# A first batch rearranged: the order of its steps, its filler matmuls, the banks they use, and two loads for the output weights

## The chip, the cores and the metric

One core of a Trainium2 chip runs the whole kernel. The core's engines work beside each other, each on its own list of instructions in a fixed order: TensorE (matmuls into the accumulator memory PSUM), VectorE (DVE in the profile), ScalarE (ACT), GpSimd (POOL, which issues most loads here) and SyncE (SP, which issues stores and transposing transfers). An instruction that needs another engine's result, or a buffer that another engine still reads, waits on a semaphore, and everything behind it on its own engine waits too. The metric is the device time of one execution in microseconds (us), as a median of several.

## The reference

The kernel computes Linformer attention and then a gated feed-forward layer. There are 8 batches, 8 heads of 64 and 1024 positions:

```python
k_proj = np.einsum('ks,bhsd->bhkd', E, k)
v_proj = np.einsum('ks,bhsd->bhkd', F, v)
scores = scale * np.matmul(q, k_proj.transpose(0, 1, 3, 2))
attn = softmax(scores)                        # over 64 projected positions
x = matmul(attn, v_proj)                      # as 8192 rows of 8 x 64 = 512
out = (sigmoid(x @ w_gate) * (x @ w_val)) @ w_out
```

E and F project 1024 positions to 64. w_gate and w_val are 512 x 1536, w_out is 1536 x 512. All inputs are float32; the kernel's loads turn them to bfloat16.

## The kernel before

The feed-forward layer is most of the work. It runs on blocks of 512 rows, two blocks to a batch, and its operand is xT, the attention's output transposed into four slices of 128 columns (i = 0 to 3). From the second batch on, a planner (`arranged`, L58) puts instructions in order by estimated costs and due times. The first batch, which the change touches, is written out by hand (L1865 to L2010): the order of the calls is the order on each engine.

The first batch's first block is handled in two halves of the heads, R = 0 (heads 0 to 3) and R = 1 (heads 4 to 7), since the loads come in halves. `start_loads` (L472) issues on GpSimd, in this order: k R=0, q R=0, k R=1, q R=1, v R=0, v R=1, then the weights in chunks. Loads are served one after the other. The steps of one half are:

- `k_part(R)`: `project` (16 matmuls with E into one bank), then `keep_k`, a cast to SBUF by ScalarE (L660).
- `qt(R, engines)`: q is transposed by TensorE into two banks, each copied out by the engine named (L715).
- `turn_k`: transposes the projected k, then a copy by ScalarE to kpD (L686).
- `sc(R)`: scores into two banks; ScalarE writes their exponentials to eT (L738).
- `den(R)`: sums of the exponentials by matmul with a selection matrix, then a RECIPROCAL on VectorE (L764, L780).
- `bc(R)`: spreads the reciprocals over partitions by float32 matmuls into two banks; the calls `keep(0)` and `keep(1)` let ScalarE copy them to xu (L797).
- `v_part(R)`: `project` with F into two banks, then four casts to vpD, two on ScalarE and two on VectorE (`keep_v`, L670).
- `xo(R)`: attention times v into two banks, then VectorE scales them by xu into xT (L843): two instructions of 512 columns for R = 0 (`scale`, L829), four of 256 for R = 1 (L869).

After these, `first_pair` (L1256) begins the feed-forward layer with the pair m = 0, 1 of its twelve column groups, on slices i = 0 and 1 (heads of R = 0), runs xo(1) in between, and goes on to slices 2 and 3. `mstep` and the rest follow; the output projection `oproj` (L1312) reads w_out (tile wO) first at 72.0 us. wO is one load, issued on GpSimd once two transposes of q have landed (L1912).

`busy(n)` (L628) issues n filler matmuls of 128x512. Their result is read by nobody; they go to PSUM bank F3, and like every writer of a bank they wait for whoever still reads what stood in it.

PSUM has eight banks, A0 to A3 and F0 to F3. In the first block the steps take banks from one list in the order of their calls, `whole` (L358); `first_pair` then uses F0 to F3. The program records for each bank who wrote and read it, and emits a wait where an engine comes to a bank that another has not yet finished with (`Plan.add`, L154).

```python
    + (A2, A3, F0, A0, A1, F1)      # the list before, its second line: k, q, q, turn_k, sc, sc
```

Of the kernel before, what the change touches and what calls it, by code (L numbers as in the profile page):

```python
# [12 lines left out]
P = 128  # L13
# [224 lines left out]
def bass_linformer_attn__then__ffn_glu_sigmoid_kernel(  # L238
# [18 lines left out]
    with contextlib.ExitStack() as es:  # L257
# [89 lines left out]
        class Ring:  # L347
# [9 lines left out]
        F0, F1, F2, F3 = FB  # L357
        whole = Ring(  # L358
            (A0, A1)
            + (A2, A3, F0, A0, A1, F1)  # L360
            + (A2, F2, A3, A0, F0)
            + (A2, A3, A1, F1, F2)
            + (A0, F0, A1, F1, A2, A3)
            + (A0, F3, A2, A3)
        )
        ffn, att = Ring(FB), Ring(AB)

# [289 lines left out]
                        tp=(0, 64 * h),  # L657
                    )

        def keep_k(bk, c0, R=None):  # L660
            width = 256 if R is None else 128
            act(
                kp[:, pairs(R), :],
                bank[bk][:, c0 : c0 + width],
                [],
                [("kp", x) for x in both(R)],
                b=bk,
            )

        def keep_v(bks, c0, engines, R=None):  # L670
            vv = vpD[:, :, :].rearrange("p (r h) d -> p r h d", h=2)
            width = 256 if R is None else 128
            for n, (h, g) in enumerate(((0, 0), (1, 1), (0, 1), (1, 0))):
                o = vv[64 * g : 64 * g + 64, pairs(R), h, :]
                i = bank[bks[h]][64 * h : 64 * h + 64, c0 : c0 + width].rearrange(
                    "p (r d) -> p r d", d=DH
                )
                ws = [("vpD", h, g, x) for x in both(R)]
                if engines[n] == "ACT":
                    act(o, i, [], ws, b=bks[h])  # L680
                else:
                    dve(lambda e, o=o, i=i: e.tensor_copy(o, i), [], ws, b=bks[h])  # L682

        def turn_k(ring, R=None):
            bk = ring.next()
            ob = bank[bk][:, :].bitcast(BF16)  # L686
            rs = range(NR)[pairs(R)]
            for n, r in enumerate(rs):
                for g in range(2):
                    mm(  # L690
                        bk,
                        ob[64 * g : 64 * g + 64, n * P : (n + 1) * P],
                        kp[:, r, :],
                        ident[:, :],
                        [("kp", r // 2), "ident"],
                        tr=True,
                        tp=(0, 64 * g),
                    )
            act(
                kpD[:, 2 * rs[0] : 2 * rs[-1] + 2, :].rearrange("p h c -> p (h c)"),  # L700
                ob[:, 0 : P * len(rs)],
                [],
                [("kpD", x) for x in both(R)],
                b=bk,
            )

        def VPD(R):
# [2 lines left out]
        def half_unit(hf, ring):  # L710
# [4 lines left out]
            def qt(R, engines):  # L715
                for rr, eng in enumerate(engines):
                    bk = ring.next()
                    ob = bank[bk][:, :].bitcast(BF16)
                    for x in range(2):
                        for t in range(2):  # L720
                            c = x * 2 + t
                            mm(
                                bk,
                                ob[:, c * P : (c + 1) * P],
                                Qb[:, 4 * R + 2 * rr + x, (2 * hf + t) * P : (2 * hf + t + 1) * P],
                                ident[:, :],
                                [("Q", hf, R), "ident"],
                                tr=True,
                            )
                    o = qv[:, R, 2 * rr : 2 * rr + 2, 256 * hf : 256 * hf + 256]  # L730
                    i = ob[:, 0:512].rearrange("p (x c) -> p x c", x=2)
                    ws = [("qT", hf, R, rr)]
                    if eng == "ACT":
                        act(o, i, [], ws, b=bk)
                    else:
                        dve(lambda e, o=o, i=i: e.tensor_copy(o, i), [], ws, b=bk)

            def sc(R):  # L738
                bks = [ring.next(), ring.next()]
# [103 lines left out]
            def xo(R):  # L843
                bks = [ring.next(), ring.next()]
                for rr in range(2):
                    for g in range(2):
                        for c in range(2):
                            h = 4 * R + 2 * rr + c
                            kk = slice(64 * (g ^ c), 64 * (g ^ c) + 64)
                            mm(  # L850
                                bks[g],
                                bank[bks[g]][64 * c : 64 * c + 64, 256 * rr : 256 * rr + 256],
                                vpD[kk, h, :],
                                eT[kk, 2 * R + g, 256 * rr : 256 * rr + 256],
                                VPD(R) + [("eT", 2 * R + g)],
                                tp=(64 * (g ^ c), 64 * c),
                            )
                for g in range(2):
                    n = 2 * R + g
                    if hf:  # L860
                        act(xu[:, n, :], bank[bks[g]][:, :], [], [("xu", n)], b=bks[g])
                    elif R == 0:
                        scale(R, g, bank[bks[g]], xu[:, n, :], [("xu", n)], bks[g])
                if hf == 0 and R == 1:
                    for r in (2, 3):
                        for g in range(2):
                            cc = slice(256 * (r - 2), 256 * (r - 2) + 256)
                            dve(
                                lambda e, r=r, g=g, cc=cc: e.tensor_tensor(  # L869
                                    xT[s][:, r, hf, 256 * g : 256 * g + 256],  # L870
                                    bank[bks[g]][:, cc],
                                    xu[:, 2 * R + g, cc],
                                    ALU.mult,
                                ),
                                [("xu", 2 * R + g)],
                                [("xT", s, r, hf, g)],
                                b=bks[g],
                            )
# [377 lines left out]
        def first_pair(blk, between):  # L1256
# [3 lines left out]
                for i in ii:  # L1260
                    mm_one(blk, m, i, n, pbs[m, n])

            step(0, "G", 0, 1)
            step(1, "G", 0, 1)
            if between:
                between()
            step(0, "V", 0, 1)
# [44 lines left out]
        def oproj(blk, tt, pb, cols=((0, DM),)):  # L1312
# [3 lines left out]
            for n, (c0, c1) in enumerate(cols):  # L1316
                if n:
                    pb = FF.take()
                for m in range(NF):
                    mm(  # L1320
                        pb,
                        bank[pb][:, 0 : c1 - c0],
                        hT[blk % 2][:, m, tt * P : (tt + 1) * P],
                        wO[:, m, c0:c1],
                        [("hT", blk % 2, m, tt // 2), "wO", "wO12"],
                        start=(m == 0),
                        stop=(m == NF - 1),
                    )
# [22 lines left out]
        def t_sums(n):  # L1351
# [1 line left out]
            B21, B22 = wO[:, H6:NF, 0:256], wO[:, H6:NF, 256:512]  # L1353
            T4, T3, T2 = [wT[:, i, :, :] for i in range(3)]
            o, a, b, op, r, w = {
                3: (T3, B22, B12, ALU.subtract, ["wO", "wO12"], [("wT", 3)]),
                2: (T2, T3, B11, ALU.add, ["wO", ("wT", 3)], [("wT", 2)]),
                4: (T4, B21, T2, ALU.subtract, ["wO", ("wT", 2)], [("wT", 4)]),
                1: (B12, B12, B11, ALU.subtract, ["wO"], ["wO12", ("wT", 1)]),
            }[n]  # L1360
            if n == 4:
                w = w + ["bsel8", ("kp", 0), ("kp", 1)]
# [28 lines left out]
        def product(blk, bk, A, B, start=False, stop=False, js=(0, 1), ms=(0, NF // 2), also=()):  # L1391
            h = hT[blk % 2]
            for j in js:
                for m in range(*ms):
# [7 lines left out]
                    elif B[0] == "T":  # L1402
                        rhs, k = wT[:, 4 - int(B[1]), m, :], ("wT", int(B[1]))
                    else:
                        c = 256 * (B[2] == "2")
                        rhs, k = wO[:, m + H6 * (B[1] == "2"), c : c + 256], "wO"
                    mm(
                        bk,
                        bank[bk][:, 256 * j : 256 * j + 256],
# [459 lines left out]
        busy(5)  # L1869
        qt, sc, den, bc, xo = half_unit(0, whole)  # L1870

        def k_part(R):
            bk = whole.next()
            project(0, 0, [bk, bk], 0, R)
            keep_k(bk, 0, R)

        def v_part(R):
            bks = [whole.next(), whole.next()]
            project(1, 1, bks, 0, R)
            keep_v(bks, 0, ["ACT", "DVE", "ACT", "DVE"], R)  # L1880

        k_part(0)
        qt(0, ("DVE", "DVE"))
        turn_k(whole, 0)
        busy(1)
        sc(0)
        busy(2)
        k_part(1)
        den(0)
        turn_k(whole, 1)  # L1890
        busy(1)
        qt(1, ("ACT", "DVE"))
        busy(1)
        sc(1)
        keep = bc(0)
        keep(0)
        keep(1)
        den(1)
        v_part(0)
        busy(1)  # L1900
        xo(0)
        keep = bc(1)
        keep(0)
        v_part(1)
        keep(1)

        def second_loads():
# [1 line left out]
            load_k(1)  # L1909
            load_v(1)  # L1910
            transpose_q()
            load(  # L1912
                wO[:, :, :],
                moe_w_out.rearrange("(m p) c -> p m c", p=P),
                ["wO", "wO12"],
                "wO",
                r=turned()[:2],
            )


        todo, at = [], {}
# [200 lines left out]
```

## Time and profile before

| what | value |
| --- | --- |
| median of 8 runs | 518.69 us (518.47 to 519.29) |
| the profiled execution's own time | 518.55 us |
| its span | 516.8 us |
| TensorE busy | 504.8 us (98%) |
| VectorE busy | 409.8 us (79%) |
| ScalarE busy | 345.5 us (67%) |
| first feed-forward matmul | starts at 21.98 us |
| load of w_out | issued at 57.37 us, 13.5 us to landing |

The span is the time between the first and the last instruction of the profiled execution; its own time includes what lies around that. Times of rows are counted from the span's start. A row has a group of equal instructions: the tile written, the tiles read, partitions by elements, and how many. The tiles' names leave numbers out, so that pA is any of A0 to A3 and pF any of F0 to F3. Some small tiles of the first batch live inside larger ones that are used later: the reciprocals and the identity matrix stand under gT, the projected k under wT, the selection patterns under vT.

### The profile page before, as it was taken

How to read it: one execution, taken by the hardware profiler on the slowest of the kernel's cores; microseconds unless marked ns; L12 is line 12 of the kernel's file. 1: busy time of each engine (PE TensorE's matmuls, PEld its weight loads, DVE VectorE, ACT ScalarE, POOL GpSimd, SP SyncE). 2: the span in 40 equal slices, each digit the busy share in tenths (PEclk: the TensorE clock that was granted, in tenths of full speed). 3: DMA queues.
4: the chain of work that ended last, by engine and by line, in shares of the span. 5: the costliest groups of instructions: out<-in, count | busy, mean ns of one | idle time of the engine just before them, and what ended most of it. 6: DMA issues, size and time to landing. Idle time of an engine off the chain costs nothing.

```text
span 516.8 us, 11359 instructions
## 1 busy us (share of the span) xinstructions
PE 504.8 (98%) x4595; PEld 410.4 (79%) x4595; DVE 409.8 (79%) x806; ACT 345.5 (67%) x646; POOL 40.4 (8%) x59
## 2 busy tenths in 40 slices
PE   4899999999999999999999999999999999999997
PEld 2545645888888888888888888888888888888885
DVE  4448789889779796987879887797968898786775
ACT  2565682867777767676767676777677766676752
POOL 9420201200200020000200020000000000000000
PEclk9999999999999999999999999999999999999999
DMA  9999999899599779364957379374104330201013
GB/s 166 199 199 203 149 199 211 121 177 223 79 214 171 162 134 155 63 160 127 158 87 163 63 139 205 67 154 92 64 1 103 42 103 1 82 2 62 20 42 124
DMA packets 105189, 63.13 MB, mean 122 GB/s; under 512 B 63024, under 2 KB 97328, under 8 KB 105136
## 3 DMA queue, kind: packets, MB, share of 16 engines
q0 software_dynamic: 33984, 29.89, 37.5%
q1 hardware_dynamic: 71152, 32.52, 28.3%
q8 instruction: 36, 0.59, 0.5%
q14 instruction: 17, 0.14, 0.1%
HBM read 60.29 MB, written 16.78 MB: 149 GB/s over the span
## 4 chain that ended last, share of the span: by engine, by line
PE 94%; DMA 2%; DVE 1%; ACT 1%; POOL 0%; issue 0%; DVEq 0%; POOLq 0%
PE pA L385 51%; PE pF L385 43%; DMA KVs<-in_k_dram 2%; DVE hT L1830 0%; DVE vsnap L1708 0%; ACT vpD L389 0%; ACT vsnap L389 0%; DVE gT L780 0%; POOL KVs L403 0%; DVE vpD L682 0%; POOL Qb L403 0%; DVE ost L1435 0%; ACT sig L389 0%; DVE sig L1784 0%; ACT xu L389 0%
## 5 line engine op out<-in xcount | busy, mean ns | idle before, releaser
L389 ACT ACTIVATE sig<-pA 128x512 f32<-128x512 f32 x126 | 75.1, 596 | 46.0 <-PE pA L385 45.7
L1697 ACT ACTIVATE pF<-pA 128x512 f32<-128x512 f32 x99 | 58.6, 591 | 35.2 <-PE pA L385 30.1
L1708 DVE TENSOR_TENSOR vsnap<-pF,vsnap 128x512 f32<-128x512 f32 x90 | 61.7, 686 | 18.0 <-ACT vsnap L389 9.4
L1784 DVE TENSOR_TENSOR sig<-pF,sig 128x512 f32<-128x512 f32 x84 | 57.6, 686 | 4.3 <-PE pA L385 2.7
L385 PE MATMUL pF<-wO,hT 128*128 128x256 bf16 (+1 forms) x402 | 59.4, 285 | 0.0
L1830 DVE SCALAR_TENSOR_TENSOR hT<-sig,vsnap 128x512 bf16<-128x512 f32 x84 | 56.7, 685 | 1.0
L389 ACT ACTIVATE vsnap<-pA 128x512 f32<-128x512 f32 x84 | 50.1, 597 | 8.1 <-PE pA L385 7.8
L389 ACT ACTIVATE sig<-sig 128x512 f32<-128x512 f32 x84 | 52.7, 628 | 2.9 <-DVE sig L1784 2.5
L385 PE MATMUL pF<-xS,wV 128*128 128x256 bf16 x360 | 54.0, 273 | 0.1
L1830 DVE SCALAR_TENSOR_TENSOR hT<-sig,pF 128x512 bf16<-128x512 f32 x42 | 28.7, 684 | 30.5 <-PE pF L385 30.0
L385 PE MATMUL pA<-xT,gT 128*128 128x256 bf16 x336 | 50.5, 273 | 0.0
L385 PE MATMUL pA<-xT,vT 128*128 128x256 bf16 x336 | 50.4, 273 | 0.0
L385 PE MATMUL pF<-xS,wG 128*128 128x256 bf16 x336 | 50.4, 273 | 0.0
L385 PE MATMUL pF<-xT,wG 128*128 128x256 bf16 (+1 forms) x264 | 50.2, 311 | 0.0
L389 ACT ACTIVATE sig<-pF 128x512 f32<-128x512 f32 x66 | 39.5, 598 | 14.9 <-PE pF L385 12.5
L385 PE MATMUL pA<-wT,hT 128*128 128x256 bf16 x360 | 48.8, 273 | 0.1
L385 PEld LDWEIGHTS pF<-wO,hT 128*128 128x128 bf16 x402 | 38.7, 98 | 10.5 <-issue 0.8
L385 PE MATMUL pF<-xT,wV 128*128 128x256 bf16 (+1 forms) x240 | 41.5, 294 | 0.0
L385 PEld LDWEIGHTS pF<-xS,wV 128*128 128x128 bf16 x360 | 34.9, 98 | 6.1 <-DVE vsnap L1708 0.4
L385 PEld LDWEIGHTS pA<-wT,hT 128*128 128x128 bf16 x360 | 34.5, 98 | 5.4 <-ACT EF L389 0.8
L389 ACT ACTIVATE eT<-pA 128x512 bf16<-128x512 f32 x59 | 34.5, 595 | 5.5 <-PE pA L385 4.9
L385 PEld LDWEIGHTS pA<-xT,gT 128*128 128x128 bf16 x336 | 31.1, 98 | 7.5 <-issue 1.9
(158 smaller groups left out, 911.0 us busy)
## 6 DMA issues: line engine op xcount, KB each, us to landing
out_dram<-ost SPq DMA_DIRECT2D x61, 256.0 KB, 2.4
Qb<-in_q_dram POOLq DMA_DIRECT2D x7, 1024.0 KB, 10.5
KVs<-in_k_dram POOLq DMA_DIRECT2D x7, 1024.0 KB, 13.3
KVs<-in_v_dram POOLq DMA_DIRECT2D x7, 1024.0 KB, 17.8
wO<-in_moe_w_out_dram POOLq DMA_DIRECT2D x1, 1536.0 KB, 13.5
wG<-in_moe_w_gate_dram POOLq DMA_DIRECT2D x5, 256.0 KB, 18.4
wV<-in_moe_w_val_dram POOLq DMA_DIRECT2D x5, 256.0 KB, 19.0
KVs<-in_k_dram POOLq DMA_DIRECT2D x2, 512.0 KB, 9.5
```

The costliest lines, as they stand in the source:

```text
L385: return add("PE", lambda e: e.matmul(o, lhsT, rhs, **kw), r=r, x=[("bank", b)])
L389: return add("ACT", lambda e: e.activation(o, i, func, scale=scale), r=r, w=w, x=x, t=t)
L1697: lambda e: e.activation(bank[c][:, :], bank[a][:, :], AF.Copy, scale=1.0),
L1708: lambda e: e.tensor_tensor(o, bank[bk][:, :], o, ALU.add),
L1784: dve(lambda e: e.tensor_tensor(o, bank[bk][:, :], o, ALU.add), [key], [key], b=bk)
L1830: lambda e: e.scalar_tensor_tensor(o, sg.rearrange("p (j c) -> p j c", j=2), 1.0, x.rearrange("p (j c) -> p j c", j=2), ALU.add, ALU.mult,),
```

## The change

The calls of the first block are put into another order. k of R = 1 is followed by qt(1) and turn_k before den(0); v_part(0) comes between the calls keep(0) and keep(1); v_part(1) comes straight after xo(0), and bc(1) after that. There are 16 fillers instead of 11, in other places. Both of k's copies for R = 1 go to VectorE, and all four casts of v for R = 1 to ScalarE. The scalings of R = 0 are four of 256 columns like those of R = 1. The first four gate matmuls go by slice, both m on slice 0 and then both on slice 1. The list of banks is a new one, fitted to the new order. wO is loaded by two transfers, m < 6 and m >= 6, with a name each for those who read them.

```diff
         whole = Ring(
             (A0, A1)
-            + (A2, A3, F0, A0, A1, F1)
-            + (A2, F2, A3, A0, F0)
-            + (A2, A3, A1, F1, F2)
-            + (A0, F0, A1, F1, A2, A3)
-            + (A0, F3, A2, A3)
+            + (A2, A3, F0, A0)
+            + (A1, F1, A2, F2, A3, A0)
+            + (F0, A2, F2)
+            + (A1, F1, A3, A0, F0)
+            + (F2, F3, A3, A0, A1, A2)
+            + (A3, A0)
         )
...
+        def copied(eng, o, i, ws, bk):
+            if eng == "ACT":
+                act(o, i, [], ws, b=bk)
+            else:
+                dve(lambda e: e.tensor_copy(o, i), [], ws, b=bk)
...
-                    elif R == 0:
-                        scale(R, g, bank[bks[g]], xu[:, n, :], [("xu", n)], bks[g])
-                if hf == 0 and R == 1:
-                    for r in (2, 3):
+                if hf == 0:
+                    for r in (2 * R, 2 * R + 1):
                         for g in range(2):
...
-            step(0, "G", 0, 1)
-            step(1, "G", 0, 1)
+            step(0, "G", 0)
+            step(1, "G", 0)
+            step(0, "G", 1)
+            step(1, "G", 1)
             if between:
                 between()
...
-                        [("hT", blk % 2, m, tt // 2), "wO", "wO12"],
+                        [("hT", blk % 2, m, tt // 2)] + (["wO0", "wO12"] if m < H6 else ["wO1"]),
...
-        k_part(0)
+        k_part(0, "ACT")
+        busy(1)
         qt(0, ("DVE", "DVE"))
         turn_k(whole, 0)
         busy(1)
         sc(0)
         busy(2)
-        k_part(1)
+        k_part(1, "DVE")
+        busy(2)
+        qt(1, ("DVE", "ACT"))
+        turn_k(whole, 1, "DVE")
         den(0)
-        turn_k(whole, 1)
-        busy(1)
-        qt(1, ("ACT", "DVE"))
         busy(1)
         sc(1)
+        busy(2)
         keep = bc(0)
         keep(0)
+        v_part(0, ["ACT", "DVE", "ACT", "DVE"])
         keep(1)
         den(1)
-        v_part(0)
         busy(1)
         xo(0)
+        v_part(1, ["ACT", "ACT", "ACT", "ACT"])
+        busy(1)
         keep = bc(1)
         keep(0)
-        v_part(1)
         keep(1)
...
-            load(
-                wO[:, :, :],
-                moe_w_out.rearrange("(m p) c -> p m c", p=P),
-                ["wO", "wO12"],
-                "wO",
-                r=turned()[:2],
-            )
+            for x, w in enumerate((["wO0", "wO12"], ["wO1"])):
+                load(
+                    wO[:, H6 * x : H6 * x + H6, :],
+                    moe_w_out.rearrange("(m p) c -> p m c", p=P)[:, H6 * x : H6 * x + H6, :],
+                    w,
+                    f"wO{x}",
+                    r=turned()[:2],
+                )
```

## The prediction

> **What bounds the kernel now.** I read the page first, then TensorE's waits in two stretches, then the rows in order of time from 13 to 26 us on TensorE, VectorE and ScalarE, and last the loads with their times to landing.
>
> ```profile
> span 516.8 us, 11359 instructions
> ...
> PE 504.8 (98%) x4595; PEld 410.4 (79%) x4595; DVE 409.8 (79%) x806; ACT 345.5 (67%) x646; POOL 40.4 (8%) x59
> ```
>
> TensorE is busy for all but 12 us of the span. Its waits from 24 us to the end, and then those of the first 24 us:
>
> ```profile
> PE pA L385 <- DVE hS L1380: 0.3, 1, 0.3
> ```
> ```profile
> PE pA L385 <- DVE vT L592: 5.9, 1, 5.9
> PE pA L385 <- DVE vpD L682: 0.7, 1, 0.7
> PE pA L385 <- DMA Qb<-in_q_dram: 0.5, 1, 0.5
> ```
>
> After the first batch nothing but 0.3 us is waited for, so whatever the first batch gives or loses reaches the end whole. The place to watch is the start of the feed-forward matmuls (21.98 us) and, after their two pauses, the first one on the third slice of xT (24.82), from which TensorE runs without a stop. TensorE's rows in order of time (start, length, then the group; the last bracket is idle time before it):
>
> ```profile
> 13.64 0.64 PE L385 MATMUL pA<-KVs,EFT 128*64 128x128 bf16 x16 [0.18 <-DMA KVs<-in_k_dram]
> 14.21 0.41 PE L385 MATMUL pF<-eT,dsel 128*32 128x128 bf16 x8
> ...
> 19.98 0.30 PE L385 MATMUL pA<-eT,vpD 64*64 64x256 bf16 x2 [0.72 <-DVE vpD L682]
> ...
> 20.32 1.16 PE L385 MATMUL pA<-gT,vT 32*128 32x128 f32 x16
> ...
> 21.98 1.04 PE L385 MATMUL pF<-xT,wG 128*128 128x512 bf16 x4
> ...
> 23.41 0.41 PE L385 MATMUL pA<-eT,vpD 64*64 64x256 bf16 x6
> ...
> 24.82 0.38 PE L385 MATMUL pF<-xT,wG 128*128 128x512 bf16 x1
> ```
>
> VectorE in the same stretch:
>
> ```profile
> 14.78 0.95 DVE L780 RECIPROCAL gT<-pF 64x128 f32<-64x128 f32 x1 [2.45 <-PE pF L385]
> ...
> 18.40 0.96 DVE L780 RECIPROCAL gT<-pF 64x128 f32<-64x128 f32 x1 [2.11 <-PE pF L385]
> 19.29 0.55 DVE L682 CAST vpD<-pF 64x128 bf16<-64x128 f32 x2
> ...
> 22.20 0.62 DVE L682 CAST vpD<-pF 64x128 bf16<-64x128 f32 x2 [0.39 <-PE pF L385]
> 23.91 1.42 DVE L869 TENSOR_TENSOR xT<-pA,xu 128x256 bf16<-128x256 f32 x4 [1.09 <-PE pA L385]
> ```
>
> A reciprocal of only 64x128 takes 0.95 us there, and VectorE waits for TensorE, not the reverse, except for 0.7 us at 19.98. The loads of the second halves, queried at their issue:
>
> ```profile
> Qb<-in_q_dram POOLq DMA_DIRECT2D x1, 256.0 KB, 11.2
> ...
> KVs<-in_v_dram POOLq DMA_DIRECT2D x1, 512.0 KB, 14.9
> ```
>
> Issued at 3.71 and 5.17 us, the second q lands at 14.93 and the second v at 20.06.
>
> **The change, part by part.** I follow the new order with durations from these rows. Up to the second k projection (13.64) only a filler is added after the first; it costs 0.22 us (fillers start at 15.00, the next row at 15.22) and lies in the 0.50 us wait for q. Cover: that load; without it, 0.22 us.
>
> *Second half of q and k.* After k_part(1) come two fillers and qt(1) instead of den(0). qt(1) now needs the load: 14.93 + 0.05 (the first q: 11.09 landed, 11.14 started) = 14.98. qt takes 0.55 to the next row (11.14 to 11.69), turn_k 0.23 (11.69 to 11.92): den(0) starts at 15.76, its reciprocal 0.57 later (14.21 to 14.78), at 16.33 instead of 14.78.
>
> The two casts of k moved to VectorE are not in the trace there. Bounds: the 64x128 cast, 0.29, and the 128x512 copy, 0.42 (ScalarE took 0.28 and 0.38). I take 0.30 each, the small cast being nearest in elements per partition for the first. The first ends by 14.75 and is hidden by qt(1); the second follows turn_k at about 15.9 and ends at 16.2 to 16.33, before the reciprocal is due. Either end costs nothing there. sc(1) starts at about 16.4 (16.30 before).
>
> *The first reciprocal.* 16.33 + 0.95 + 0.15 (VectorE's end to TensorE's start, as 19.84 to 19.98) = 17.43 for bc(0), before at 16.64. In the old order this reciprocal had finished 0.9 us before it was wanted. Two fillers in the gap cost nothing. bc takes 1.09 (20.32 to 21.41), so v_part(0) starts at 18.52 (18.30 before), v having landed at 17.53.
>
> *VectorE's queue behind v_part(0).* Projection to cast: 0.75 (18.30 to ScalarE's first cast at 19.05), 19.27. Two casts 0.65, reciprocal 0.90 until the next may start, four scalings 1.42: 19.27 + 0.65 + 0.90 + 1.42 = 22.24. Before, the order reciprocal, casts, two scalings ended at 21.81, and nothing on TensorE waited for that end. Splitting two scalings (1.29 us, 20.52 to 21.81) into four (1.42) costs 0.13 on this line.
>
> *TensorE beside it.* xo(0) starts when the second VectorE cast ends: 19.27 + 0.62 + 0.15 = 20.04 (19.98 before). It takes 0.34, v_part(1) starts at 20.38; v landed at 20.06, so that load isn't waited for. v_part(1) takes 0.57 (13.64 to 14.21) and ends at 20.95.
>
> *The filler that waits.* All fillers write PSUM bank F3. The new list of banks gives xo(0) the banks F2 and F3. So the filler between v_part(1) and bc(1) has to wait until the scalings have read F3, the last of which is the fourth: 22.24 + 0.15 = 22.39. Queued behind it on TensorE: bc(1), and all of the feed-forward stage; ScalarE's copies of bc(1) wait for those. Filler 0.22: bc(1) at 22.61 (20.32 before); 1.09: first gate matmuls at 23.70 (21.98). All scalings are done by then, so the new order of these four matmuls gains and costs nothing. They take 0.99 (21.98 to 22.97): xo(1) at 24.69.
>
> *Given back.* Before, xo(1) stood at 22.97 and waited until 23.41 for a bank that ScalarE was copying. With the new banks it needs only vpD(1). Its four casts are all on ScalarE, 4 x 0.295 after v_part(1) ends (20.38 + 0.75), done at 22.3: hidden by 2.4 us. That gains 0.44. xo(1) to its scalings 0.50 (23.41 to 23.91), two of them 0.76, 0.15 to TensorE: the third slice starts at 24.69 + 1.41 = 26.10, before 24.82. The loss is 1.28 us, say 1.3.
>
> *Output weights.* One more issue of 0.9 us on POOL, which is free from 58.4 to 59.67; without that cover the k load behind it comes 0.9 later, and its landing (75.91) is 9 us before use. The single load landed at 70.86, first use 72.01. I take nothing; the bounds are 0 and, if the second half came 0.9 late, still 0, since half m>=6 is used 1.3 us after the first.
>
> *Sum.* Profiled execution 518.55 us (span 516.8) + 1.3 = 519.85. It stands 0.14 below the median of 518.69, so the median becomes 520.0 (519.97).
>
> *A rule against it.* Here the fillers' 128x512 matmuls start 0.427 us apart before 10 us (five take 2.34 us from 7.64), 0.216 apart later, also after the 0.72 us wait at 19.98. The Trainium skill, "TensorE: Matmul & The Clock Gate", section "HAM oscillation — how this bites in real kernels", says that only idle gaps of more than about 3.4 us let the clock fall. By it fillers in such waits buy nothing and the new 1.4 us wait cools nothing: +1.3. If instead a 1.4 us wait did cool TensorE, the third rival below holds. No row shows a wait between 0.72 and 5.9 us.
>
> **The rivals.**
> 1. *The waiting filler does not cost, not slower.* If the four scalings were done before v_part(1) ends (20.95, against 22.24 + 0.15), bc(1) would wait only for the second reciprocal (20.82 + 0.15) and follow the filler at 21.18; gates at 22.27, xo(1) at 23.26, third slice 24.67: 0.15 us gained, 518.5. For it speaks that the old VectorE had 2 us idle before its reciprocal; against, that 1.3 us would have to vanish from a queue of 2.97 us whose durations all stand in rows. Chance 0.08, with larger gains a part of it.
> 2. *bc(0) is not late.* If the first reciprocal ended before sc(1) did, everything up to the filler would move 0.7 forward: +0.6, 519.3. The landing of q at 14.93 stands against it; it decides if q lands 0.7 earlier. Chance 0.08, with everything between +0.2 and +0.9.
> 3. *The clock falls in the wait.* Cold TensorE lasted from 5.9 to about 10 us. If 4 us after 22.4 ran at half pace, 2 us more, at most: 520.0 + 2.0 = 522. Against it: the fillers and v_part(1) ran up to 20.95. Chance 0.06.
>
> **How the numbers follow.** My forecast has 0.78. Its own uncertainty is some 0.3 us: bounds of the two casts (0.1 each if they reach the reciprocal), the hand-overs of 0.04 to 0.15, and landings. So 519.5 to 520.6; below, rival 2 to 519.0; above, part of rival 3 to 521.0. That leaves out rival 1, the rest of 3, and tails. About 0.2% (1.04 us) is what a measurement of this kernel tells from no change; my 1.3 is not far above it. Slower by more than that, over 519.73: 0.82 of the forecast's 0.78 and all of rival 3: 0.70. Within: the other 0.14 of the forecast, rival 2's 0.08 and 0.05 of rival 1: 0.27. Faster, the larger gains of rival 1: 0.03.
>
> **What would show it.** In the profile after: a TensorE wait of about 1.4 us for xT's scalings just before a filler near 22.4; bc(0) near 17.4, released by the reciprocal; no wait for v; xo(1) without its 0.44 wait; third slice near 26.1; no TensorE wait later. I am wrong if the filler's wait is short, if matmuls after it start 0.427 apart, or if a later wait takes the delay up.

## The result, and the profile after

The changed kernel takes 521.97 us (median of 12 runs, 519.54 to 523.02), the kernel before 518.51 us on the same chip (median of 32, 517.53 to 519.29). The ratio is 1.0064, with a 95% interval from 1.0055 to 1.0073. It is slower, by more than twice what I forecast, and the time lies above my range.

The twelve runs do not lie around one value. Sorted by TensorE's mean granted clock, which is recorded for every run, they make three groups:

| mean granted clock | runs | times, us |
| --- | --- | --- |
| 1.000 | 1 | 519.54 |
| 0.996 to 0.997 | 5 | 521.02 to 521.45 |
| 0.993 | 6 | 522.50 to 523.02 |

The execution that was profiled is the one at 1.000, with its own time of 519.54 us. It lies 0.3 us under my forecast of 519.85 for such an execution, and by itself it hides what happened in the other eleven. It is read first, to see whether the steps came as forecast. The head of its page, and TensorE's waits up to 24 us and after:

```profile
span 517.7 us, 11372 instructions
...
PE 506.3 (98%) x4600; PEld 410.5 (79%) x4600; DVE 410.1 (79%) x808; ACT 345.7 (67%) x646; POOL 41.1 (8%) x60
```
```profile
PE pA L386 <- DMA EF<-in_F_dram: 5.7, 1, 5.7
PE pF L386 <- DVE xT L868: 1.4, 1, 1.4
PE pF L386 <- DVE vpD L665: 0.3, 1, 0.3
PE pA L386 <- ACT kpD L390: 0.2, 1, 0.2
```
```profile
PE pA L386 <- DVE hS L1381: 0.3, 1, 0.3
```

(5.7 us is the wait for the first loads.) The waits for q and for vpD that stood at 0.5 and 0.7 us are nearly gone. In their place is one wait of 1.4 us for the scalings that write xT. From 24 us on nothing but the old 0.3 us is waited for. TensorE's rows in order of time (start, length, group; the bracket is idle time before it and what ended it):

```profile
19.41 0.41 PE L386 MATMUL pF<-eT,vpD 64*64 64x256 bf16 x8 [0.26 <-DVE vpD L665]
19.75 0.64 PE L386 MATMUL pA<-KVs,EFT 128*64 128x128 bf16 x16
...
21.77 0.39 PE L386 MATMUL pF<-gT 128*128 128x512 bf16 x1 [1.37 <-DVE xT L868]
22.08 1.16 PE L386 MATMUL pA<-gT,vT 32*128 32x128 f32 x16
23.18 1.04 PE L386 MATMUL pF<-xT,wG 128*128 128x512 bf16 x4
24.14 0.41 PE L386 MATMUL pA<-eT,vpD 64*64 64x256 bf16 x8
...
25.62 0.38 PE L386 MATMUL pF<-xT,wG 128*128 128x512 bf16 x1
```

The third row is one filler. It stands idle for 1.37 us, until VectorE has read bank F3 out, and bc(1) and the feed-forward matmuls stand behind it. VectorE's rows of the same execution:

```profile
14.14 0.29 DVE L665 CAST wT<-pA 128x128 bf16<-128x128 f32 x1 [1.85 <-PE pA L386]
15.34 0.29 DVE L665 COPY kpD<-pA 128x256 bf16<-128x256 bf16 x1
15.76 0.95 DVE L781 RECIPROCAL gT<-pF 64x128 f32<-64x128 f32 x1
...
20.29 1.42 DVE L868 TENSOR_TENSOR xT<-pF,xu 128x256 bf16<-128x256 f32 x4
```

The four scalings run from 20.29 to 21.71, and the filler starts 0.06 us later. The third slice of xT is used at 25.62. This execution's loads landed some 0.6 us earlier than those of the profile before (the second q at 14.36, not 14.93). Counted from that landing the third slice came 11.26 us after it, and I had forecast 26.10 - 14.93 = 11.17.

So the delay is what I said, where I said. What is left is that eleven of twelve runs are 1.5 to 3.5 us slower than this one, at a lower mean clock.

### The profile page after: what moved, and what is told of

The parts are those of the page before. It is cut to its first block, busy times and chain, and to the rows that moved or that the text cites. A ratio compares the mean times of both kernels' runs of the same rounds, so it can differ in the third digit from the quotient of the medians.

```text
span 517.7 us, 11372 instructions
## 1 busy us (share of the span) xinstructions
PE 506.3 (98%) x4600; PEld 410.5 (79%) x4600; DVE 410.1 (79%) x808; ACT 345.7 (67%) x646; POOL 41.1 (8%) x60
## 4 chain that ended last, share of the span: by engine, by line
PE 96%; DVE 2%; DMA 1%; ACT 1%; issue 0%; SPq 0%; DVEq 0%
PE pA L386 52%; PE pF L386 44%; DMA EF<-in_F_dram 1%; DVE hT L1831 0%; DVE vsnap L1709 0%; DVE xT L868 0%; ACT vsnap L390 0%; DVE vpD L665 0%; ACT vpD L390 0%; DVE ost L1436 0%; ACT sig L390 0%; DVE sig L1785 0%; SPq L477 0%; DVE ost L1521 0%; ACT kpD L390 0%
```

## The experiments

Two explanations stood against each other. The theory: the idle time in front of that filler costs twice, once as a delay of 1.0 to 1.4 us, and again because TensorE then runs at half its clock for a stretch, in the runs where the clock is below 1. The rival: the loss beyond the delay comes from another part of the change, such as the two loads of wO, the split scalings or the order of the gate matmuls, or from a clock that falls whatever this wait does. Each ratio below is against runs of the kernel before on the same chip, made together with it; their medians were 518.77, 518.47 and 518.81 us.

### The changed kernel, a second profile

No edit. This was to catch one of the executions at a lower clock in a profile.

> The changed kernel once more, for a second profile. Its twelve times lie near three levels, 519.5, 521.2 and 522.7 us, with a mean granted clock of 1.000, 0.997 and 0.993. Theory A (the clock falls in the wait before the filler in bank F3): the profile shows a stretch of half clock that begins between 20 and 27 us, some 3.4 us long or twice that, in which 128x512 matmuls start 0.427 us apart; the span is 1.6 or 3.2 us longer than 517.7. Theory B (the levels come from the loads, which land at other times): the clock row stays at 1.00 and the landings of q and v are later by the difference. If the run happens to be a fast one (519.5), it tells nothing.

It took 521.38 us, at a mean clock of 0.996. TensorE's rows:

```profile
22.16 0.39 PE L386 MATMUL pF<-gT 128*128 128x512 bf16 x1 [1.37 <-DVE xT L868]
...
23.57 1.70 PE L386 MATMUL pF<-xT,wG 128*128 128x512 bf16 x4
...
25.77 1.73 PE L386 MATMUL pF<-xT,wV 128*128 128x512 bf16 x4
...
27.34 0.38 PE L386 MATMUL pF<-xT,wG 128*128 128x512 bf16 x1
```

The wait is the same 1.37 us. But the four gate matmuls take 1.70 us, where the undisturbed execution showed 1.04. A table by stretches shows where (stretch, length, then each engine's busy time with its instructions, PEclk as a share of the full clock, and the DMA's share and rate):

```profile
20.38:23.79 3.41, 2.04 (x34) 1.42 (x29) 1.69 (x5) 1.21 (x5) 0.00 (x0) 1.00 1.44 195
23.79:27.20 3.41, 3.41 (x16) 1.06 (x15) 1.23 (x4) 0.96 (x2) 0.00 (x0) 0.50 1.45 197
27.20:30.60 3.40, 3.40 (x17) 1.40 (x15) 1.52 (x3) 1.59 (x3) 0.00 (x0) 1.00 1.45 195
```

The clock is 1, then 0.50 for 3.41 us, then 1 again. Within that stretch the gate matmuls start 0.43 us apart (24.21 and 24.64 us), the sign by which the prediction said that it would be wrong. TensorE is busy through all of the slow stretch, so it loses half of it, 1.7 us. The stretch of 3.41 us just before it holds the wait: 1.37 us of it are idle.

### The waiting filler, given a bank that is free

```diff
-        def busy(n):
+        def busy(n, b=FB[3]):
...
-                    FB[3],
-                    bank[FB[3]][:, :].rearrange("p (a c) -> p a c", a=4),
+                    b,
+                    bank[b][:, :].rearrange("p (a c) -> p a c", a=4),
...
         v_part(1, ["ACT", "ACT", "ACT", "ACT"])
-        busy(1)
+        busy(1, A1)
```

> Only the bank of the one filler between v_part(1) and bc(1) is changed, from F3 to A1, which no engine still reads then. Theory A (the wait for the scalings delays the batch, and its idle time lets the clock fall): no wait of 1.37 us; bc(1) waits only for the second reciprocal; third slice of xT 1.3 to 1.6 us earlier than the 25.62 of the changed kernel's profile, so about 24.1; clock 1.000 in all runs; 517.9 to 518.4 us, ratio to the kernel before 0.998 to 1.000. Theory B (the rest of the rearrangement costs the time): 521 to 522 us and scattered, as the changed kernel.

It took 518.84 us (518.47 to 519.72, 11 runs), ratio 1.0003 with an interval from 0.9994 to 1.0011. All eleven runs had a clock of 0.999 or 1.000. The bank of one filler carries the whole loss: delay and clock are both gone. The small gain that I expected on top did not show. In the profiled run, which with 519.72 us is the longest of the eleven, v landed late and took part of it; for the other ten no profile says why:

```profile
21.43 0.64 PE L386 MATMUL pA<-KVs,EFT 128*64 128x128 bf16 x16 [0.82 <-DMA KVs<-in_v_dram]
22.00 0.39 PE L386 MATMUL pA<-gT 128*128 128x512 bf16 x1
```

The filler now follows v_part(1) without a wait; that projection itself waited 0.82 us for its load.

### The wait left in place, but filled

To part delay from clock, the waiting filler stays, and six fillers that wait for nothing go ahead of it. TensorE then works while VectorE scales.

```diff
         v_part(1, ["ACT", "ACT", "ACT", "ACT"])
+        busy(6, A1)
         busy(1)
```

> The wait stays: the filler in bank F3 still comes after the scalings, but six fillers in bank A1 (6 x 0.216 = 1.3 us) are put ahead of it, so that TensorE works through the 1.37 us. Theory A: third slice still at about 25.6, but no fall of the clock: 519.3 to 519.9 us in all runs, ratio 1.0015 to 1.0025. Theory C (the levels come from the delay itself, whatever TensorE does in it): 519.5 to 523 us in three levels, as the changed kernel, ratio about 1.006.

```profile
20.25 1.47 PE L386 MATMUL pA<-gT 128*128 128x512 bf16 x6
21.69 0.39 PE L386 MATMUL pF<-gT 128*128 128x512 bf16 x1
```

It took 520.11 us (519.51 to 520.89, 9 runs), ratio 1.0028 (1.0018 to 1.0038), all at a clock of 0.999 or 1.000. The delay is there, some 1.45 us (0.0028 of 518.8), a little above the ratio of 1.0015 to 1.0025 that I expected; the clock no longer falls. The difference to the changed kernel, 1.0064 against 1.0028, is the clock's share. Theory C falls: the delay alone makes no levels.

### The waiting filler left out

```diff
         v_part(1, ["ACT", "ACT", "ACT", "ACT"])
-        busy(1)
```

> The one filler between v_part(1) and bc(1) is left out; no work of the result is. Theory A: as with the filler in A1 or up to 0.2 us better, since bc(1) then starts as soon as the second reciprocal is done: 517.7 to 518.4 us, ratio 0.9975 to 1.000, clock 1.000. Theory D (this filler keeps the clock up): half clock in some runs, 519.5 us or more there.

518.64 us (518.03 to 519.42, 11 runs), ratio 1.0000 (0.9991 to 1.0009). All eleven runs had a clock of 0.999 or 1.000, so it was not this filler that kept the clock up. A changed kernel without it is as fast as the kernel before; the median lies just above the 517.7 to 518.4 us that I expected, and the small gain did not come here either. The other fillers, the new order and the new banks together neither gain nor lose.

### The parts of the change that move no step

The kernel before, with wO in two loads, four scalings for R = 0 and the gate matmuls by slice; the order of the steps, the banks and the fillers stay those of before.

```diff
-                if hf == 0 and R == 1:
-                    for r in (2, 3):
+                if hf == 0:
+                    for r in (2 * R, 2 * R + 1):
...
-            step(0, "G", 0, 1)
-            step(1, "G", 0, 1)
+            step(0, "G", 0)
+            step(1, "G", 0)
+            step(0, "G", 1)
+            step(1, "G", 1)
...
-            load(
-                wO[:, :, :],
...
+            for x, w in enumerate((["wO0", "wO12"], ["wO1"])):
+                load(
+                    wO[:, H6 * x : H6 * x + H6, :],
...
```

> The kernel before with only the parts of the change that move no step: w_out in two loads, four scalings instead of two for R = 0, the gate matmuls by slice. My prediction took nothing for each. Theory A: ratio 0.999 to 1.001. A rival (the second load of w_out pushes the loads behind it, or the 0.13 us of scalings come on the path): ratio 1.001 to 1.003, and a wait of TensorE for w_out near 72 us.

518.48 us (517.96 to 520.23, 12 runs), ratio 1.0005 (0.9996 to 1.0015). These parts cost nothing that can be measured. The rival that put the loss there falls.

### How much idle time lets the clock fall

One filler, and in another kernel three, ahead of the one that waits, so that the idle time shrinks while the delay stays.

```diff
         v_part(1, ["ACT", "ACT", "ACT", "ACT"])
+        busy(1, A1)     # the other kernel: busy(3, A1)
         busy(1)
```

> As the kernel whose wait was kept warm, but with one filler in bank A1 ahead of the waiting filler instead of six: about 1.15 us of the wait are left idle. In the second profile of the changed kernel, the 3.41 us before the clock fell had TensorE busy for 2.04 us, idle for 1.37; in the kernel before no such stretch had more than 0.8 us idle, and the clock stayed up. Theory A (idle time within one such stretch decides): most runs still fall, 521 to 523 us, perhaps fewer than the eleven of twelve of the changed kernel. If the limit lies above 1.15 us, 519.8 to 520.5 us as with six.

> Three fillers in bank A1 ahead of the waiting one: about 0.7 us of the wait are left idle, as much as the kernel before had at 19.98 us. Theory A: no fall, 519.6 to 520.5 us, mean clock 0.999 to 1.000. Theory E (any wait at this place lets the clock fall unless it is filled whole): some runs at 521 us and more.

With one filler, 519.73 us (518.84 to 521.14, 8 runs), ratio 1.0025 (1.0013 to 1.0037). I expected most runs to fall, and only one of eight did, the one that was profiled. It shows how close to the limit it was:

```profile
21.84 0.39 PE L386 MATMUL pF<-gT 128*128 128x512 bf16 x1 [1.05 <-DVE xT L868]
```
```profile
19.26:22.67 3.41, 2.13 (x34) 1.35 (x36) 2.46 (x6) 1.68 (x5) 0.03 (x1) 1.00 1.46 195
22.67:26.09 3.42, 3.42 (x24) 1.47 (x22) 0.00 (x0) 1.08 (x2) 0.00 (x0) 0.50 1.45 195
```

With three, 519.62 us (518.90 to 520.09, 10 runs), ratio 1.0022 (1.0013 to 1.0031), and none fell; its wait was 0.62 us:

```profile
21.50 0.39 PE L386 MATMUL pF<-gT 128*128 128x512 bf16 x1 [0.62 <-DVE xT L868]
```

Both kernels still pay the delay, about 1.2 us (0.0022 to 0.0025 of 518.5), because the filler that waits still stands in the queue. What three fillers ahead of it remove is the fall of the clock. Theory E, that any idle rest of the wait brings the clock down, does not hold.

Where the limit lies can be bounded from the profiles of this study. The clock changes only at the ends of stretches of 3.41 us that follow one another without a gap. For each such stretch at full clock, the idle time is 3.41 less TensorE's busy time. The stretches of the first batch nearest to the limit on both sides:

| execution | stretch, us | idle, us | clock of the next stretch |
| --- | --- | --- | --- |
| before | 10.14 to 13.55 | 0.79 | 1.00 |
| waiting filler in A1 | 19.65 to 23.06 | 1.08 | 1.00 |
| changed, profiled first | 17.94 to 21.35 | 1.21 | 1.00 |
| one filler ahead | 19.26 to 22.67 | 1.28 | 0.50 |
| changed, second profile | 20.38 to 23.79 | 1.37 | 0.50 |
| changed, third profile | 20.61 to 24.02 | 1.49 | 0.50 |
| before, without its fillers between steps | 10.66 to 14.07 | 1.60 | 0.50 |

In the first batch the line runs between 1.21 and 1.28 us, that is some 36% of a stretch. TensorE's busy time is a modelled figure, so the third digit should not be trusted.

The line does not hold for the whole kernel. At its end, when TensorE has done its last matmul, the kernel before has a stretch with 1.75 us of idle time, and the clock stays up in the next:

```profile
511.90:515.32 3.42, 1.67 (x16) 1.25 (x13) 1.64 (x4) 0.60 (x1) 0.00 (x0) 1.00 0.55 188
515.32:516.76 1.44, 0.00 (x0) 0.00 (x0) 0.00 (x0) 0.00 (x0) 0.00 (x0) 1.00 0.28 99
```

The same holds at the end of the changed kernel's first profile (1.75 us) and of the kernel before without its fillers (1.60), while 2.34 us at the end of the changed kernel's second profile brought the clock down. So idle time is not all that decides. One difference that the rows show: all 16 matmuls of the stretch above are 128*128, whereas of the 34 in the changed kernel's stretch from 20.38 to 23.79, 32 are 32*128 or 128*64 and use only a part of the array. Whether that is what counts was not tested.

The changed kernel's first profile, at full clock throughout, has the same 1.37 us wait, but the border at 21.35 cut it in two:

```profile
17.94:21.35 3.41, 2.20 (x49) 1.37 (x49) 2.61 (x7) 2.52 (x7) 1.32 (x2) 1.00 1.44 195
21.35:24.76 3.41, 3.00 (x31) 1.67 (x32) 0.40 (x3) 1.39 (x4) 0.00 (x0) 1.00 1.45 195
```

Idle time of 1.21 and 0.41 us, and both stretches stay under the line. Where the borders lie differs between executions (17.94 here, 20.38 and 20.61 in the two others). That accounts for these three executions, one at full clock and two with a fall.

### The changed kernel, a third profile

No edit. It was to catch a run of the group at 0.993.

> The changed kernel a third time, to see an execution of the slowest level (522.7 us, mean clock 0.993) if it comes. Theory A: half clock for two stretches of 3.41 us instead of one, the first of them beginning inside or before the wait for the scalings, so that the second is decided by a stretch that still has idle time; span 520.9. With one stretch only, as in the second profile: 519.4, and nothing new.

It took 521.66 us at 0.996, and again had one stretch at half clock:

```profile
20.61:24.02 3.41, 1.92 (x33) 1.46 (x29) 1.73 (x5) 1.17 (x5) 0.00 (x0) 1.00 1.45 196
24.02:27.43 3.41, 3.34 (x15) 1.02 (x15) 1.15 (x4) 1.00 (x2) 0.00 (x0) 0.50 1.45 195
```

The group at 0.993 was not caught. One stretch at half clock takes 3.41 x 0.5 / 519 = 0.0033 off the mean clock, so 0.9967 is one stretch and 0.9934 is two. The times agree: 1.7 us and 3.4 us above some 519.4. That the six runs at 0.993 had two stretches is worked out, and no profile shows where the second lay.

### The kernel before, without its fillers between the steps

The five fillers at the start stay; the six between the steps go. This asked whether fillers in short waits do anything, in a kernel where no filler waits for a bank.

```diff
         turn_k(whole, 0)
-        busy(1)
         sc(0)
-        busy(2)
         k_part(1)
         den(0)
         turn_k(whole, 1)
-        busy(1)
         qt(1, ("ACT", "DVE"))
-        busy(1)
         sc(1)
...
         v_part(0)
-        busy(1)
         xo(0)
```

> The kernel before without the six fillers between the steps of the first batch (the five at its start stay). None of them is on a result. Counted from its trace, the stretch of 3.41 us from 10.14 would have 1.65 us of idle time without its fillers, 0.79 with them; one from 17 us 1.05 instead of 0.72. Theory A (more than some 1.1 us of idle time in such a stretch lets the clock fall): most runs have half clock for 3.4 us or more, 519.5 to 522 us, ratio 1.002 to 1.007. By the Trainium skill's rule, 'TensorE: Matmul & The Clock Gate', only idle gaps over 3.4 us cool: same as before or 0.2 us less, ratio 0.999 to 1.001.

522.04 us (517.23 to 522.66, 10 runs), ratio 1.0035 (1.0010 to 1.0059). Again two groups: four runs at a clock of 1.000 (517.23 to 518.64) and six at 0.987 (522.03 to 522.66). The profile is one of the six. Its longest waits in the stretch before the fall, and the stretches:

```profile
PE pA L385 <- DMA KVs<-in_k_dram: 0.7, 1, 0.7
PE pA L385 <- ACT kpD L389: 0.5, 1, 0.5
PE pA L385 <- DMA Qb<-in_q_dram: 0.4, 1, 0.4
```
```profile
10.66:14.07 3.41, 1.81 (x38) 1.12 (x36) 0.76 (x2) 1.52 (x4) 3.41 (x6) 1.00 1.32 202
14.07:17.48 3.41, 3.15 (x44) 2.00 (x38) 1.38 (x2) 1.48 (x4) 3.41 (x6) 0.50 1.24 206
17.48:20.90 3.42, 3.42 (x40) 2.85 (x40) 0.74 (x1) 2.17 (x4) 1.78 (x3) 0.50 1.41 197
...
24.31:27.73 3.42, 3.09 (x29) 1.44 (x28) 0.59 (x2) 1.73 (x4) 0.00 (x0) 0.50 1.45 196
27.73:31.14 3.41, 3.34 (x19) 1.24 (x16) 1.98 (x5) 1.14 (x2) 0.00 (x0) 1.00 1.45 196
```

No wait there is longer than 0.7 us, but 1.60 us together were enough for the clock to fall. Here the sum within a stretch counted, not the longest gap. The old kernel's fillers, which I had taken to buy nothing, keep about 4 us in six runs of ten: none of the 21 runs of the kernel before beside these had a clock under 0.999.

### A version of my own: the first reciprocal early again

The profiles showed two places where the new order loses time: den(0) behind qt(1), which makes bc(0) wait for its reciprocal, and the waiting filler. This version keeps the new places of the two v_part steps, puts den(0) back ahead of turn_k and qt(1), drops the filler between v_part(1) and bc(1) and the two pairs after k_part(1) and after sc(1), copies k of R = 1 on ScalarE as before, shares v's casts, and has a list of banks to fit.

```diff
-            + (A2, A3, F0, A0)
-            + (A1, F1, A2, F2, A3, A0)
-            + (F0, A2, F2)
-            + (A1, F1, A3, A0, F0)
-            + (F2, F3, A3, A0, A1, A2)
-            + (A3, A0)
+            + (A2, A3, F0, A0, A1, F1)
+            + (A2, F2, A3, A0, F0)
+            + (A2, A3, A1, F1)
+            + (A0, F0, F2, A2, A3)
+            + (A0, F3, A1, F1, A2, A3)
...
-        k_part(1, "DVE")
-        busy(2)
-        qt(1, ("DVE", "ACT"))
-        turn_k(whole, 1, "DVE")
+        k_part(1, "ACT")
         den(0)
+        turn_k(whole, 1)
+        qt(1, ("ACT", "DVE"))
         busy(1)
         sc(1)
-        busy(2)
...
-        v_part(1, ["ACT", "ACT", "ACT", "ACT"])
-        busy(1)
+        v_part(1, ["ACT", "DVE", "ACT", "DVE"])
```

> A version of my own: the changed kernel with den(0) put back ahead of the second half of q (its reciprocal is then done before bc(0) wants it), k of R = 1 copied by ScalarE again, no filler between v_part(1) and bc(1), casts of v for R = 1 shared again, and banks chosen so that no step waits for a bank of which it doesn't need the contents. Worked out as in the prediction: bc(0) at about 16.6, v_part(0) at 17.7, xo(0) 19.3, v_part(1) at the landing of v (20.1), bc(1) 20.7, gates 21.8, third slice 24.15 where the kernel before has 24.82: 518.0 us, ratio 0.998 to 0.9995. Rival: TensorE's own work from v's landing on (0.57 + 1.09 + 0.99 + 0.34 + 0.87 = 3.86 us) and the landing bound it, so that nothing is gained over leaving the filler out: ratio 0.9995 to 1.001.

VectorE's first reciprocal, and TensorE's first matmuls on the first and the third slice of xT:

```profile
14.78 0.95 DVE L780 RECIPROCAL gT<-pF 64x128 f32<-64x128 f32 x1 [2.29 <-PE pF L385]
```
```profile
21.11 1.04 PE L385 MATMUL pF<-xT,wG 128*128 128x512 bf16 x4
...
23.55 0.38 PE L385 MATMUL pF<-xT,wG 128*128 128x512 bf16 x1
```

517.67 us (517.08 to 520.40, 12 runs), ratio 0.9986 (0.9974 to 0.9998). The third slice comes at 23.55, before at 24.82; but v of R = 1 landed earlier too, at 19.40 and not 20.06. Counted from that landing it comes after 4.15 us, before after 4.76 us, and in the kernel without the filler after 4.37 us (24.63, v at 20.26). It is faster than both kernels, against the one before by some 0.7 us, which is at the edge of what the measurement tells from no change. Which of its differences from the kernel without the filler gains this was not tested: v_part(1) starts at 19.45, 0.05 us after its load, so from there on the landing bounds it, as the rival said. One run of its twelve had a clock of 0.993 and took 520.40.

To see whether more filling removes that run, one more filler went ahead of sc(1) and one ahead of xo(0):

```diff
         qt(1, ("ACT", "DVE"))
-        busy(1)
+        busy(2)
         sc(1)
...
-        busy(1)
+        busy(2)
         xo(0)
```

> The version with the early reciprocal, and two fillers instead of one ahead of sc(1) and of xo(0), where its profile had 0.25 us and 0.26 us of idle time left (and some more that the rows hide). One of its twelve runs had a mean clock of 0.993 (520.4 us). Theory A: the same median, 517.5 to 518.0, ratio 0.998 to 0.9995, and no run with a clock under 0.998; if the added fillers overshoot, 0.1 to 0.2 us more.

518.24 us (517.32 to 522.10, 11 runs), ratio 0.9994 (0.9978 to 1.0009). One run of eleven is still at 0.993. The fillers did not remove it. By the two ratios they cost some 0.4 us against the version without them, which is not a difference that these intervals separate. Where the clock falls in those single runs stays open. Single falls are not special to this version: of the 79 runs of the kernel before that were made beside the experiments, one had a clock of 0.997 (519.72 us).

## Why the prediction was wrong, and where it was right

The loss, taken as a mean over the twelve runs, is 0.0064 x 518.5 = 3.3 us. By the runs it divides so:

| part | forecast, us | measured, us | from |
| --- | --- | --- | --- |
| delay behind the waiting filler | 1.3 | 1.2 to 1.45 | the kernels with three and six fillers ahead; 1.0 in the one run at full clock |
| half clock after the wait | 0 | about 2.0 | 3.3 less the delay; counted as 1.7 us a stretch, one in five runs and two in six, it would be 2.4 |
| everything else | 0 | none that can be measured | the free bank, the filler left out, the parts alone |

**What failed** is the step "A rule against it", and with it the chance of the third rival. No row of the trace before showed a wait between 0.72 and 5.9 us, as I wrote, so the trace could not say what a 1.4 us wait does. I let a rule decide: the Trainium skill, "TensorE: Matmul & The Clock Gate", section "HAM oscillation — how this bites in real kernels", gives as the rule "no PE-idle gaps >~3.4µs". That shorter gaps therefore do nothing was my reading of it. The runs contradict that reading. In the first batch the clock fell when the longest gap was 1.05 or 1.37 us, and also when no gap was over 0.7 us, once the idle time of one stretch came to 1.28 us or more. That put at 0 a cost of about 2.0 us a run. What the same page's section "What's actually happening" says of a window of 3413 ns that runs freely agrees with the 3.41 us measured. Had I taken that window together with the row, a wait of 1.4 us in 3.41 would have been 40% idle, and nothing on record made so low a chance as 0.06 safe.

**The third rival** named the right mechanism. That its 522 meets the median of 521.97 is luck: no run lies there, and the median falls between the group near 521.2 and the one near 522.7. Its argument against itself, that the fillers and v_part(1) ran up to 20.95, does not hold. By the table of stretches, work done before a stretch begins does not count for it, and the stretch from 20.38 to 23.79 began only 0.4 us before that work ended (22.16 - 1.37 = 20.79). Its "4 us at half pace, 2 us more" was one stretch of 3.41 us, 1.7 us, or, by the mean clock of six runs, two.

**The filler that waits.** Right, in place, cause and size. In the profile after, it waited 1.37 us (forecast 1.4) for the fourth scaling, and bank F3 alone made it wait: with A1 the loss was gone. As times from the landing of the second q, forecast and measured: first reciprocal 1.40 and 1.40, v_part(0) 3.59 and 3.50, xo(0) 5.11 and 5.05, end of the scalings 7.31 and 7.35, filler 7.46 and 7.41, gate matmuls 8.77 and 8.82. The largest misses cancelled: the hand-over from VectorE to TensorE took 0.06 us and not 0.15, and filler to bc(1) 0.31 and not 0.22.

**The first reciprocal** was late as forecast: it ended at 16.71, and bc(0) followed at 16.77; the forecast "near 17.4" less the 0.57 us of earlier loads is 16.86. Rival 2 did not hold, since the reciprocal did decide bc(0) although q landed 0.57 earlier.

**The two casts of k** took 0.29 us each (I took 0.30), hidden as said. **xo(1)** had no wait: the 0.44 us came back. **Scalings, gate order and wO** cost nothing, as forecast; the kernel with these parts alone measured 1.0005. **Rival 1**, that the filler's wait costs nothing, did not hold; but its sum was tested by giving the filler a free bank. It said 0.15 us gained, and 1.0003 (0.9994 to 1.0011) can't tell that from no change.

**The range** reached only to 521.0, because the 0.06 bought no room for the 522 that I had worked out. A row missing between 0.72 and 5.9 us was an unknown cost with the ends 0 and 2 us, and the range should have held both.

## What to carry to other kernels

Look at which buffer a filler writes: it waits like any other instruction, and everything behind it waits too. A filler belongs in a bank that nobody reads at that moment, ahead of the instruction that will wait. Where TensorE's waits in a stretch of some 3.4 us add up to over a third of it, as here in the first batch, a fall of the clock can add another 1.7 us or more. Allow for that in the range, and look at the granted clock of every run before trusting one profile: here the profiled execution was the one in twelve in which the clock had not fallen.

## What the runs showed of the hardware

- The granted clock changed only at the ends of stretches of 3.41 us, between 1.00 and 0.50. Their borders lay elsewhere in each execution, so that the same 1.37 us wait left the clock up in one profile (519.54 us) and brought it down in another (521.38 us).
- In the first batch, idle time of up to 1.21 us in a stretch left the clock up; 1.28 to 1.60 us brought it down for the next stretch, whether mostly in one gap or in several. At the kernel's end 1.75 us left it up and 2.34 us brought it down. What besides idle time counts is open.
- Once down it did not always come up after one stretch. In the kernel before without its fillers, the clock stayed at 0.50 for four stretches, though TensorE was busy for 3.15 and 3.42 us of the first two. What decides the return is open.
- With all those stretches at half clock, from 14.07 to 27.73, that run lost only some 4 us against the four at full clock, not 13.66 / 2 = 6.8. Probably TensorE would otherwise have spent part of that time waiting; no run here separates this.
